# Loading the first head's K in pairs, and a running elementwise maximum, in a decode step with a gated MLP

## The chip, the cores and the metric

The kernel runs on one core of a Trainium2 chip. The metric is device time in microseconds for one execution. The span in the profile is the part from the first to the last recorded instruction of the kernel; a little time lies around it.

## The reference

One token of width 1024 goes through two branches that are mixed by a scalar gate. Branch A is attention against a long cache: 32 query heads share 4 K/V heads, 65536 cached positions, head width 128. Branch B is a small gated MLP.

```python
g = sigmoid((x * gate_w).sum(-1, keepdims=True))
# branch A
q = (x @ wq).reshape(B, Sq, 32, 128).transpose(0, 2, 1, 3)
k = repeat(k_cache, 8, axis=1)            # k_cache: (1, 4, 65536, 128), bf16
v = repeat(v_cache, 8, axis=1)
p = softmax(einsum('bhqd,bhkd->bhqk', q, k) * 128 ** -0.5)
a = einsum('bhqk,bhkd->bhqd', p, v).reshape(B, Sq, 4096) @ wo
# branch B
z = gelu(einsum('bsd,df->bsf', B_x, w_in))
z2 = layernorm(z[..., Fh:])
b = einsum('bsf,fd->bsd', z[..., :Fh] * (einsum('ts,bsf->btf', w_sp, z2) + b_sp), w_out)
out = g * a + (1 - g) * b                 # (1, 1, 1024) bf16
```

K and V are 67 MB each, so the kernel reads 162 MB from HBM in all and writes 2 KB.

## The kernel before

All large inputs pass through one SBUF tensor, `kv`, with five slots of 32 KB per partition (4 MB in all for a slot). `load` (its `dma_start` is L184) issues every one of these transfers from SP, in program order, and `load_kv(src, g, j, at, n)` loads n neighbouring tiles of K or V of head g into the slots from `at` on. A transfer waits on SP until the slots it overwrites have been read; the transfers behind it wait too. One head of K is four tiles of 4 MB, one of V is four as well. The last loop over instructions in the kernel adds an order dependence between neighbours on each engine, so that each engine runs its instructions in the order in which the program writes them.

In this text K00 to K03 are the four K tiles of head 0; K(g) h=0 and K(g) h=1 are the transfers of two K tiles of head g, and V(g) h=0 and V(g) h=1 those of V.

`k_tile(g, j, kn)` makes the scores of one K tile. In four parts, VectorE (DVE) transposes a part in place (L403, 128x2048 of int32) and TensorE (PE) multiplies it with the spread-out query `wt` (L410, 8 matmuls a part) into `s_ps`. ScalarE (ACT) copies the 128x1024 scores to a bf16 tile `sc` (L421). The tile's row maximum is taken on DVE, 128x1024 to one column of a 128x4 tile `mx` (L405); it is put into the list `late` and issued behind the first transpose of the next K tile. There are five `sc` buffers.

`stats(g)` ends the maximum of a head: the last tile's reduce (L425), the reduce over the 4 columns to `m1` (L427), a PE transpose to `mt_ps`, two small DVE steps, a PE broadcast to `nb_ps`, and `nb` (L439), minus the scaled maximum. Then ACT takes Exp of the four `sc` tiles with their sums (L443), and DVE transposes each into `pt` (L446). `v_tile(g, j, vt)` multiplies a tile of V with `pt` (L456, 32 matmuls a tile) into `o_ps`, and `head_out(g)` reduces `o_ps` to the head's part of the output vector. `build_w(g)` writes the query of head g into one of two `wt` tiles (L388, 4 DVE instructions).

The order at the start: `w_in` is loaded to slots 3 and 4, `wq` to slots 0 and 1; the MLP's first product (`z_ps`) reads the one, the query's (`q_ps`) the other. Then:

```python
    build_w(0)
    for j, n, at in ((0, 1, 2), (1, 1, 3), (2, 1, 0), (3, 1, 1)):
        for i, kn in enumerate(load_kv(A_k_cache, 0, j, at, n)):
            k_tile(0, j + i, kn)
        if j == 1:
            build_w(1)
    project(load(B_w_out.rearrange("(p c) n -> p c n", c=FC), (FC, D), 4), FC, uT, 0, first=True)
    stats(0)
```

So K00 is in slot 2, K01 in slot 3, K02 in slot 0, K03 in slot 1, the MLP's output weights in slot 4. For each head g from 1 on, the loop over h then loads a pair of K tiles of head g (slots 2 and 3 for h=0, slots 3 and 4 for h=1), makes their scores (for h=0 the second tile first, so that slot 3 comes free early), loads a pair of V tiles of head g-1 into slots 0 and 1 and multiplies them, with `stats(g)` between them for h=1. After the last head come the V tiles of head 3 and the output projection with `wo`.

Of the kernel before, what the change touches and what calls it, by code (L numbers as in the profile page):

```python
# [8 lines left out]
FP32 = mybir.dt.float32  # L9
BF16 = mybir.dt.bfloat16  # L10
I32 = mybir.dt.int32
ACT = mybir.ActivationFunctionType
ALU = mybir.AluOpType
AX = mybir.AxisListType

P = 128
CT = 128
NKV = 5
B = 32
NB = P // B  # L20
VC = 4
CC = CT // VC
# [7 lines left out]
def kernel(  # L30
# [15 lines left out]
    nc = tc.nc  # L46

    _, _, D = A_x.shape
    _, G, S, DH = A_k_cache.shape
# [9 lines left out]
    NT = S // (P * CT)  # L59
# [9 lines left out]
    wk = ctx.enter_context(tc.tile_pool(name="wk", bufs=2))  # L69
    big = ctx.enter_context(tc.tile_pool(name="big", bufs=1))  # L70
# [118 lines left out]
    def load_kv(src, g, j, at, n=1):  # L189
        h, i = divmod(j, 2)  # L190
        rows = src[0, g, 2 * h * CT * P:2 * (h + 1) * CT * P, :].rearrange(
            "(p c) d -> p (c d)", c=2 * CT)
        v = load(rows[:, i * CT * DH:(i + n) * CT * DH], (n * CT * DH,), at)
        return [v[:, i * CT * DH:(i + 1) * CT * DH] for i in range(n)]
# [115 lines left out]
    for hf in range(2):  # L310
# [30 lines left out]
                            op=ALU.subtract)  # L341
# [44 lines left out]
    def build_w(g):  # L386
        for v in range(VC):
            nc.vector.tensor_tensor(  # L388
                out=wt[g % 2][:, v, :, :, v, :],
                in0=qs[:, g].unsqueeze(2).to_broadcast([P, BP, NB, REP]),  # L390
                in1=own_n[:].unsqueeze(1).unsqueeze(3).to_broadcast([P, BP, NB, REP]),
                op=ALU.mult)
# [2 lines left out]
    late = []  # L395
    sct, ptt, mxs, lss, o_ps = {}, {}, {}, {}, {}

    def k_tile(g, j, kn):
        kb = kn.bitcast(I32)
        n = CC * DH // 2  # L400
        s_ps = pss.tile([P, 2 * HN], FP32, name="s_ps", tag="s")
        for v in range(VC):
            nc.vector.transpose(out=kb[:, v * n:(v + 1) * n], in_=kb[:, v * n:(v + 1) * n])  # L403
            while late:
                nc.vector.reduce_max(**late.pop())  # L405
            kx = kn[:, v * CC * DH:(v + 1) * CC * DH].rearrange(
                "p (c h k e) -> p h e c k", h=2, k=B, e=2)
            for b in range(BP):
                for k in range(2):
                    ins = nc.tensor.matmul(  # L410
                        s_ps[:, k * HN:(k + 1) * HN],
                        lhsT=wt[g % 2][:, v, b].rearrange("p a v h -> p (a v h)"),
                        rhs=kx[:, b // 2, b % 2, k * CC // 2:(k + 1) * CC // 2, :],
                        start=(v == 0 and b == 0), stop=(v == VC - 1 and b == BP - 1),
                        skip_group_check=True)
                    if k > 0:
                        same_weights(ins)
        if g not in mxs:
            mxs[g] = wk.tile([P, NT], FP32, name="mx")
        sct[g, j] = scp.tile([P, CC * B], BF16, name="sc")  # L420
        nc.scalar.copy(out=sct[g, j][:], in_=s_ps[:])  # L421
        late.append(dict(out=mxs[g][:, j:j + 1], in_=sct[g, j][:], axis=AX.X))

    def stats(g):
        nc.vector.reduce_max(**late.pop())  # L425
        m1 = wk.tile([P, 1], FP32, name="m1")
        nc.vector.reduce_max(out=m1[:], in_=mxs[g][:], axis=AX.X)  # L427
        mt_ps = psm.tile([1, P], FP32, name="mt_ps", tag="m")
        nc.tensor.transpose(mt_ps[:], m1[:], ident_f[:])
        gm = wk.tile([1, REP], FP32, name="gm")  # L430
        nc.vector.tensor_reduce(out=gm[:], in_=mt_ps[:].rearrange("p (a h) -> p h a", h=REP),
                                axis=AX.X, op=ALU.max)
        gr = wk.tile([1, P // REP, REP], FP32, name="gr")
        nc.vector.tensor_copy(out=gr[:], in_=gm[:].unsqueeze(1).to_broadcast([1, P // REP, REP]))
        nb_ps = psm.tile([P, 1], FP32, name="nb_ps", tag="m")
        nc.tensor.matmul(nb_ps[:], lhsT=gr[:].rearrange("p a h -> p (a h)"),
                         rhs=ones_f[0:1, 0:1], start=True, stop=True)
        nb = wk.tile([P, 1], FP32, name="nb")
        nc.vector.tensor_scalar(out=nb[:], in0=nb_ps[:], scalar1=-SCALE, scalar2=None,  # L439
                                op0=ALU.mult)  # L440
        lss[g] = wk.tile([P, NT], FP32, name="ls")
        for j in range(NT):
            nc.scalar.activation(out=sct[g, j][:], in_=sct[g, j][:], func=ACT.Exp, scale=SCALE,  # L443
                                 bias=nb[:, 0:1], accum_out=lss[g][:, j:j + 1])
            ptt[g, j] = ptp.tile([P, CC, B], BF16, name="pt")
            nc.vector.transpose(out=ptt[g, j][:].rearrange("p c x -> p (c x)"),  # L446
                                in_=sct[g, j][:])

    def v_tile(g, j, vt):
        if j == 0:  # L450
            o_ps[g] = pso.tile([P, 2, VC * DH], FP32, name="o_ps")
        vx = vt.rearrange("p (v c d) -> p c v d", v=VC, d=DH)
        for u in range(CC // 2):
            hs = slice(u % 2 * P // 2, (u % 2 + 1) * P // 2)
            for e in range(2):
                ins = nc.tensor.matmul(  # L456
                    o_ps[g][hs, e, :],
                    lhsT=ptt[g, j][:, 2 * u:2 * u + 2, :].rearrange("p c x -> p (c x)"),
                    rhs=vx[:, 2 * u + e], start=(j == 0 and u < 2),
                    stop=(j == NT - 1 and u >= CC // 2 - 2), skip_group_check=True)  # L460
                if e > 0:
                    same_weights(ins)

    def head_out(g):
        gs = slice(g * B, (g + 1) * B)
        nc.vector.tensor_tensor(  # L466
            out=om8, in0=o_ps[g][:].rearrange("p e (v d) -> p (e v) d", d=DH),
            in1=own_8[:].unsqueeze(2).to_broadcast([P, 2 * VC, DH]), op=ALU.mult)
        o_sb = wk.tile([P, DH], FP32, name="o_sb")
        nc.vector.tensor_reduce(out=o_sb[:], in_=om8.rearrange("p x d -> p d x"), axis=AX.X,  # L470
                                op=ALU.add)
        om_ps = psm.tile([P, DH + NT], FP32, name="om_ps", tag="m")
        hs = hsel[:].rearrange("p h q -> p (h q)")
        nc.tensor.matmul(om_ps[gs, DH:], lhsT=hs, rhs=lss[g][:], start=True, stop=True,
                         skip_group_check=True)
        nc.tensor.matmul(om_ps[gs, :DH], lhsT=hs, rhs=o_sb[:], start=True, stop=True,  # L476
                         skip_group_check=True)
        rl = wk.tile([P, 2], FP32, name="rl")
        nc.vector.reduce_sum(out=rl[gs, 0:1], in_=om_ps[gs, DH:], axis=AX.X)
        nc.vector.reciprocal(out=rl[gs, 1:2], in_=rl[gs, 0:1])  # L480
        om = wk.tile([P, QD, OC], FP32, name="om")
        nc.vector.tensor_tensor(
            out=om[gs], in0=om_ps[gs, :DH].rearrange("p (q c) -> p q c", c=OC),
            in1=own_q[gs, :].unsqueeze(2).to_broadcast([B, QD, OC]), op=ALU.mult)
        osum = wk.tile([P, OC], FP32, name="osum")
        nc.vector.tensor_reduce(out=osum[gs, :], in_=om[gs].rearrange("p q c -> p c q"),  # L486
                                axis=AX.X, op=ALU.add)
        nc.vector.tensor_scalar(out=oa[gs, :], in0=osum[gs, :], scalar1=rl[gs, 1:2],
                                scalar2=gate[gs, :], op0=ALU.mult, op1=ALU.mult)
# [22 lines left out]


    build_w(0)
    for j, n, at in ((0, 1, 2), (1, 1, 3), (2, 1, 0), (3, 1, 1)):
        for i, kn in enumerate(load_kv(A_k_cache, 0, j, at, n)):
            k_tile(0, j + i, kn)
        if j == 1:
            build_w(1)
    project(load(B_w_out.rearrange("(p c) n -> p c n", c=FC), (FC, D), 4), FC, uT, 0, first=True)  # L520
    stats(0)
    for g in range(1, G):
        for h in range(2):
            kn = load_kv(A_k_cache, g, 2 * h, 2 + h, 2)
            for i in ((1, 0), (0, 1))[h]:
                k_tile(g, 2 * h + i, kn[i])
            if h == 0 and g + 1 < G:
                build_w(g + 1)
            vn = load_kv(A_v_cache, g - 1, 2 * h, 0, 2)
            v_tile(g - 1, 2 * h, vn[0])  # L530
            if h == 1:
                stats(g)
            v_tile(g - 1, 2 * h + 1, vn[1])
        head_out(g - 1)
    for j, n, at in ((0, 2, 2), (2, 1, 1), (3, 1, 0)):
        for i, vt in enumerate(load_kv(A_v_cache, G - 1, j, at, n)):
# [59 lines left out]
```

## Time and profile before

| what | value |
|---|---|
| median of 4 runs | 382.32 us (382.15 to 382.48) |
| the profiled execution | 382.48 us, of which its span is 381.0 us |
| PE busy | 233.2 us (61% of the span) |
| DVE busy | 218.5 us (57%) |
| ACT busy | 39.6 us (10%) |
| DMA | 162.17 MB, 426 GB/s in the mean |

The times on each line of the profile come from one execution. Busy time is summed over an engine's instructions, and the engines work beside each other. In the slices each digit is the busy share of a fortieth of the span, in tenths. A group's row gives line, engine, operation, tile and shape, the count, then busy time and mean ns of one, then the engine's idle time ahead of it and what ended it. A timeline row gives start, duration, engine, line, operation, tile and count. Times are counted from the span's start.

### The profile page before, as it was taken

Reading aid. Unit: us, or ns where it says so; the run is one execution under the profiler, and the core shown is the slowest. Engines: PE = TensorE matmul, PEld = TensorE weight load, DVE = VectorE, ACT = ScalarE, POOL = GpSimd, SP = SyncE. Lnnn points to the kernel's source line nnn. Section 1 sums busy time; section 2 is a strip of 40 time slices with the busy share of each in tenths; the row PEclk is TensorE's granted clock in tenths of the full one; section 3 lists DMA queues with packets and bytes.
Section 4 is the critical chain, followed back from the end, with each engine's and each line's share of the span. In section 5 each row is a group of like instructions: output and inputs, shape, how many; then the busy total and the mean of one; then the engine's idle time right before and its main releaser. Section 6 shows DMA issues by size and latency. Waiting matters only on the chain.

```text
span 381.0 us, 2607 instructions
## 1 busy us (share of the span) xinstructions
PE 233.2 (61%) x1397; PEld 55.9 (15%) x800; DVE 218.5 (57%) x211; ACT 39.6 (10%) x55; POOL 4.4 (1%) x10
## 2 busy tenths in 40 slices
PE   0060557876257933786397729771977196839386
PEld 0010111111111200111011101120211021202113
DVE  4134298997597506966977059659970398460040
ACT  1001001110601100114010101050101000400000
POOL 4000000000000000000000000000000000000000
PEclk9995769899859995989688958895889579969789
DMA  9998999999999999999999999999999999999995
GB/s 385 482 440 375 408 441 437 437 475 443 414 413 413 440 435 433 433 440 440 440 435 433 440 440 433 435 420 393 440 440 435 433 420 434 440 404 440 454 408 216
DMA packets 3943, 162.17 MB, mean 426 GB/s; under 512 B 472, under 2 KB 476, under 8 KB 860
## 3 DMA queue, kind: packets, MB, share of 16 engines
q1 hardware_dynamic: 3892, 162.01, 98.7%
q8 instruction: 8, 0.13, 0.1%
q14 instruction: 3, 0.02, 0.0%
q10 hardware_dynamic: 40, 0.01, 0.0%
HBM read 162.01 MB, written 0.00 MB: 425 GB/s over the span
## 4 chain that ended last, share of the span: by engine, by line
DMA 57%; PE 26%; DVE 13%; ACT 2%; issue 1%; SPq 1%; DVEq 0%; ACTq 0%
DMA kv<-in_A_k_cache_dram 42%; PE s_ps L410 21%; DMA kv<-in_A_wo_dram 7%; DVE kv L403 7%; DMA kv<-in_A_v_cache_dram 7%; PE o_ps L456 4%; DVE pt L446 2%; DVE o_sb L470 1%; DVE mx L405 1%; ACT sc L421 1%; ACT sc L443 1%; DVE rowt L466 1%; SPq L184 1%; PE om_ps L476 0%; DVE osum L486 0%
## 5 line engine op out<-in xcount | busy, mean ns | idle before, releaser
L410 PE MATMUL s_ps<-kv,wt 128*128 128x512 bf16 x512 | 141.2, 435 | 80.8 <-DVE kv L403 80.8
L403 DVE STREAM_TRANSPOSE kv<-kv 128x2048 int32<-128x2048 int32 x64 | 142.7, 2280 | 53.5 <-DMA kv<-in_A_k_cache_dram 53.5
L456 PE MATMUL o_ps<-kv,pt 128*64 128x512 bf16 x512 | 61.9, 400 | 7.4 <-DMA kv<-in_A_v_cache_dram 7.4
L410 PEld LDWEIGHTS <-wt 128*128 128x128 bf16 x256 | 27.5, 108 | 195.7 <-issue 138.7
L421 ACT CAST sc<-s_ps 128x1024 bf16<-128x1024 f32 x16 | 16.2, 1013 | 249.9 <-PE s_ps L410 249.9
L456 PEld LDWEIGHTS <-pt 128*64 128x64 bf16 x256 | 16.1, 115 | 50.5 <-issue 48.1
L446 DVE STREAM_TRANSPOSE pt<-sc 128x1024 bf16<-128x1024 bf16 x16 | 18.6, 1217 | 6.8 <-ACT sc L443 6.8
L405 DVE TENSOR_REDUCE mx<-sc 128x1 f32<-128x1024 bf16 x12 | 14.5, 1209 | 10.7 <-ACT sc L421 10.7
L443 ACT ACTIVATE sc<-sc,nb 128x1024 bf16<-128x1024 bf16 x16 | 18.2, 1137 | 12.2 <-DVE nb L439 12.2
L466 DVE TENSOR_TENSOR rowt<-o_ps,own 128x1024 f32<-128x1024 f32 x4 | 4.8, 1194 | 24.9 <-PE o_ps L456 24.9
L476 PE MATMUL om_ps<-o_sb,hsel 128*32 128x128 f32 x8 | 2.3, 386 | 18.3 <-DVE o_sb L470 18.3
L425 DVE TENSOR_REDUCE mx<-sc 128x1 f32<-128x1024 bf16 x4 | 4.9, 1220 | 13.6 <-ACT sc L421 13.6
L296 PE MATMUL q_ps<-kv,xT 128*32 128x512 bf16 x64 | 5.7, 532 | 7.3 <-DMA kv<-in_A_wq_dram 7.3
L252 PE MATMUL xb_ps<-xg,spread 8*128 8x256 bf16 x1 | 0.4, 367 | 13.6 <-DMA xg<-in_gate_w_dram 13.6
L470 DVE TENSOR_REDUCE o_sb<-rowt 128x128 f32<-128x1024 f32 x4 | 7.5, 1871 | 0.1
L363 DVE TENSOR_TENSOR rowt<-q_ps,own_b 128x512 f32<-128x512 f32 x2 | 1.3, 686 | 10.9 <-PE q_ps L296 10.9
L495 PE MATMUL busy_ps<-wt 128*128 128x512 bf16 x25 | 6.1, 381 | 0.0
L296 PE MATMUL z_ps<-kv,xT 128*32 128x448 bf16 x64 | 6.1, 574 | 0.0
L256 DVE TENSOR_TENSOR xm<-xb_ps,sel_i 128x128 f32<-128x128 f32 x2 | 0.5, 286 | 8.4 <-PE xb_ps L252 8.4
L506 PE MATMUL out_ps<-kv,oa 128*32 128x256 bf16 x128 | 4.2, 273 | 1.7 <-DMA kv<-in_A_wo_dram 1.7
L552 ACT CAST out_sb<-out_ps 128x256 bf16<-128x256 f32 x1 | 0.4, 373 | 45.0 <-PE out_ps L506 45.0
L296 PEld LDWEIGHTS <-xT 128*32 128x32 bf16 x64 | 2.6, 138 | 14.7 <-issue 14.7
(90 smaller groups left out, 59.3 us busy)
## 6 DMA issues: line engine op xcount, KB each, us to landing
kv<-in_A_k_cache_dram SPq DMA_DIRECT2D x4, 4096.0 KB, 35.1
kv<-in_A_v_cache_dram SPq DMA_DIRECT2D x2, 4096.0 KB, 25.9
kv<-in_B_w_in_dram SPq DMA_DIRECT2D x1, 7168.0 KB, 19.9
kv<-in_A_wo_dram SPq DMA_DIRECT2D x1, 6144.0 KB
kv<-in_B_w_out_dram SPq DMA_DIRECT2D x1, 3584.0 KB
kv<-in_A_wo_dram SPq DMA_DIRECT2D x1, 1024.0 KB
kv<-in_A_wo_dram SPq DMA_DIRECT2D x1, 512.0 KB
kv<-in_A_wo_dram SPq DMA_DIRECT2D x2, 256.0 KB, 28.1
```

Of the source, the lines that this page charges most:

```text
L296: ins = nc.tensor.matmul(ps[t * B:(t + 1) * B, k * HN:k * HN + n], lhsT=xT[:, i * KH + c:i * KH + c + 1].to_broadcast([P, B]), rhs=w[:, c, ...
L403: nc.vector.transpose(out=kb[:, v * n:(v + 1) * n], in_=kb[:, v * n:(v + 1) * n])
L405: nc.vector.reduce_max(**late.pop())
L410: ins = nc.tensor.matmul(s_ps[:, k * HN:(k + 1) * HN], lhsT=wt[g % 2][:, v, b].rearrange("p a v h -> p (a v h)"), rhs=kx[:, b // 2, b % 2, ...
L421: nc.scalar.copy(out=sct[g, j][:], in_=s_ps[:])
L425: nc.vector.reduce_max(**late.pop())
L443: nc.scalar.activation(out=sct[g, j][:], in_=sct[g, j][:], func=ACT.Exp, scale=SCALE, bias=nb[:, 0:1], accum_out=lss[g][:, j:j + 1])
L446: nc.vector.transpose(out=ptt[g, j][:].rearrange("p c x -> p (c x)"), in_=sct[g, j][:])
L456: ins = nc.tensor.matmul(o_ps[g][hs, e, :], lhsT=ptt[g, j][:, 2 * u:2 * u + 2, :].rearrange("p c x -> p (c x)"), rhs=vx[:, 2 * u + e], sta ...
L466: nc.vector.tensor_tensor(out=om8, in0=o_ps[g][:].rearrange("p e (v d) -> p (e v) d", d=DH), in1=own_8[:].unsqueeze(2).to_broadcast([P, 2 ...
L470: nc.vector.tensor_reduce(out=o_sb[:], in_=om8.rearrange("p x d -> p d x"), axis=AX.X, op=ALU.add)
L495: ins = nc.tensor.matmul(ps[:, :HN], lhsT=w[:, :P], rhs=w[:, :HN], start=True, stop=True, skip_group_check=True)
```

## The change

Three edits. The four loads of head 0's K become two of 8 MB, into the slots that the tiles had before. `stats(0)` and the two V tiles of head 0 that V(0) h=0 brings move behind the first K tile of head 1, (1, 1), and ahead of its second, (1, 0); the order of the loads on SP stays. `build_w(2)`, and with it `build_w(3)`, comes after the V tiles of its half in the program. The row maximum of each tile is replaced by an elementwise maximum over the score tiles of a head, kept in a bf16 tile `mx` of 128x1024: the first tile is taken as it is, each further one costs one `tensor_tensor` with max, and `stats` reduces the result once along the row to `m1`.

```diff
+    mx = big.tile([P, CC * B], BF16, name="mx")
+
+    def running_max(g, sc):
+        if g in mxs:
+            nc.vector.tensor_tensor(out=mx[:], in0=mxs[g][:], in1=sc[:], op=ALU.max)
+            mxs[g] = mx
+        else:
+            mxs[g] = sc
+
     def k_tile(g, j, kn):
...
             while late:
-                nc.vector.reduce_max(**late.pop())
+                running_max(*late.pop())
...
-        if g not in mxs:
-            mxs[g] = wk.tile([P, NT], FP32, name="mx")
         sct[g, j] = scp.tile([P, CC * B], BF16, name="sc")
         nc.scalar.copy(out=sct[g, j][:], in_=s_ps[:])
-        late.append(dict(out=mxs[g][:, j:j + 1], in_=sct[g, j][:], axis=AX.X))
+        late.append((g, sct[g, j]))
 
     def stats(g):
-        nc.vector.reduce_max(**late.pop())
+        while late:
+            running_max(*late.pop())
         m1 = wk.tile([P, 1], FP32, name="m1")
         nc.vector.reduce_max(out=m1[:], in_=mxs[g][:], axis=AX.X)
...
     build_w(0)
-    for j, n, at in ((0, 1, 2), (1, 1, 3), (2, 1, 0), (3, 1, 1)):
-        for i, kn in enumerate(load_kv(A_k_cache, 0, j, at, n)):
+    for j, at in ((0, 2), (2, 0)):
+        for i, kn in enumerate(load_kv(A_k_cache, 0, j, at, 2)):
             k_tile(0, j + i, kn)
-        if j == 1:
+        if j == 0:
             build_w(1)
     project(load(B_w_out.rearrange("(p c) n -> p c n", c=FC), (FC, D), 4), FC, uT, 0, first=True)
-    stats(0)
     for g in range(1, G):
         for h in range(2):
             kn = load_kv(A_k_cache, g, 2 * h, 2 + h, 2)
-            for i in ((1, 0), (0, 1))[h]:
-                k_tile(g, 2 * h + i, kn[i])
-            if h == 0 and g + 1 < G:
-                build_w(g + 1)
+            first, then = ((1, 0), (0, 1))[h]
+            k_tile(g, 2 * h + first, kn[first])
+            early = g == 1 and h == 0
+            if early:
+                stats(0)
+            else:
+                k_tile(g, 2 * h + then, kn[then])
             vn = load_kv(A_v_cache, g - 1, 2 * h, 0, 2)
             v_tile(g - 1, 2 * h, vn[0])
             if h == 1:
                 stats(g)
             v_tile(g - 1, 2 * h + 1, vn[1])
+            if early:
+                k_tile(g, 2 * h + then, kn[then])
+            if h == 0 and g + 1 < G:
+                build_w(g + 1)
         head_out(g - 1)
```

## The prediction

> **What bounds the kernel now.** I read the slices and the DMA queue first, the chain of waits second, then the DMA share by windows.
>
> ```profile
> DMA  9998999999999999999999999999999999999995
> ...
> q1 hardware_dynamic: 3892, 162.01, 98.7%
> ...
> DMA 57%; PE 26%; DVE 13%; ACT 2%; issue 1%; SPq 1%; DVEq 0%; ACTq 0%
> ```
>
> The 16 DMA engines are busy from the first slice to the last but one. The chain gives PE 26% and DVE 13%, but it counts a transfer from its issue, also while earlier transfers are still moving, so its PE and DVE pieces lie beside a busy queue. Windows over the steady part settle it (last columns: PE clock, DMA share, GB/s):
>
> ```profile
> 110.00:180.00 70.00, 49.77 (x260) 10.87 (x131) 42.33 (x31) 8.69 (x12) 0.00 (x0) 0.87 1.00 434
> 180.00:260.00 80.00, 52.60 (x263) 11.47 (x135) 52.90 (x42) 8.69 (x12) 0.00 (x0) 0.82 1.00 432
> ```
>
> DMA share 1.00, while DVE is busy 42.3 of 70 us. The packet records agree: first large packet at 1.0 us, last end at 377.1; in between 16 packets are in flight throughout. So 376.1 of the 381.0 us are bytes over a fixed rate; start and tail are not edited. An edit moves the time only if it alters the rate or starves the queue.
>
> So the question at each load on SP is when it is issued, against when the queue runs dry:
>
> ```profile
> 45.37 0.44 SPq L184 DMA_DIRECT2D kv<-in_B_w_out_dram  x1
> 73.35 0.33 SPq L184 DMA_DIRECT2D kv<-in_A_k_cache_dram  x1
> 95.06 0.33 SPq L184 DMA_DIRECT2D kv<-in_A_v_cache_dram  x1
> 119.28 0.33 SPq L184 DMA_DIRECT2D kv<-in_A_k_cache_dram  x1
> ...
> 198.00 0.33 SPq L184 DMA_DIRECT2D kv<-in_A_k_cache_dram  x1
> ```
>
> By the packet records these five send their first packets at 76.7, 85.3, 104.6, 124.0 and 201.4: leads of 31, 11.9, 9.6, 4.7 and 3.4 us. 3.4 is the smallest in the kernel and costs nothing. The very first load goes out 1.0 us after issue, so about 1 us of lead is needed.
>
> [...] Before, single K tiles released the DVE at 49.87 and 59.66, about 1.1 us after their last packets at 48.85 and 58.53. [...] PE clock 0.50 in 108 to 112 us after 10 us idle; 32 matmuls then take 9.5 us, where warm ones take 1.9 per 8.
>
> **The change, part by part.** The rows used:
>
> ```profile
> L403 DVE STREAM_TRANSPOSE kv<-kv 128x2048 int32<-128x2048 int32 x64 | 142.7, 2280 | 53.5 <-DMA kv<-in_A_k_cache_dram 53.5
> ...
> L446 DVE STREAM_TRANSPOSE pt<-sc 128x1024 bf16<-128x1024 bf16 x16 | 18.6, 1217 | 6.8 <-ACT sc L443 6.8
> L405 DVE TENSOR_REDUCE mx<-sc 128x1 f32<-128x1024 bf16 x12 | 14.5, 1209 | 10.7 <-ACT sc L421 10.7
> ...
> L425 DVE TENSOR_REDUCE mx<-sc 128x1 f32<-128x1024 bf16 x4 | 4.9, 1220 | 13.6 <-ACT sc L421 13.6
> ```
>
> Maximum: 16 reduces of 1.21 us (19.4) and four small ones of 0.16 go; 12 elementwise maxima and 4 full reduces (4.9 us) come. [...] At the end of a head, stats is 0.5 to 1.1 us longer (maximum plus full reduce, against 1.22 + 0.16), but in heads 1 to 3 the PE transpose mt_ps queues behind 32 matmuls of v_tile (before: scores out at 171.0, m1 done at 172.4, mt_ps at 173.5), which cover it. Cost 0; if the cover went, at most 1.1 us off leads of 3.4 us or more.
>
> Pairs: four 4 MB loads become two of 8 MB; SP issues two instructions fewer (0.33 us each, beside the queue). Pair A (slots 2, 3) waits for the z matmuls, done at 26.6, where K00 waited for nothing; wq keeps the queue busy until 37.9. Pair B (slots 0, 1) waits for the q matmuls as before (44.9) and is due at 57.3. Leads of 11 and 12 us: no gap. Rate: packets of 32 KB took 38.06 ns/KB per engine, those of 64 KB 37.89. 16.8 MB are 1024 KB an engine: -0.17 us, between 0 and -0.3 (the best transfers, V pairs at 2.308 us/MB, against 2.325 for these four).
>
> Head 0, later: pair A lands as K01 did, so transposing starts at 59.7 instead of 49.9. Transposes in a row pace at 2.22 (four end in 8.9), so 8 end at 77.5. PE starts at 61.9, cold as before: 9.9 us for 32 matmuls, then 4 x 1.91, so 79.4. K(1) h=0 (slots 2, 3), issued at 73.35 before, goes at 79.4, due 85.3: lead 5.9. Pair B lands as K03 did, 78.6 + 0.5 to 1.0. One transpose (2.3) to 81.4-81.9, maximum to 82.1-83.1, four transposes (8.9) to 91.0-92.0. PE ends K02 1.9 us behind its last transpose, 90.7-91.7; the copy to sc 1.0, 91.8-92.8; maximum to 92.5-94.0; three transposes (6.7) to 99.2-100.7; PE to 101.1-102.6. So V(0) h=0 (slots 0, 1) goes at 101.1 to 102.6 instead of 95.06, due 104.6: lead 2.0 to 3.5 us instead of 9.6. This is the tight place. The 1 us needed leaves 1 to 2.5 us. Cost 0; each us past 103.6 would cost about one.
>
> Head 1, first half: K(1) h=0 lands at 106.9 as before. The PE is cold then in both kernels, so the maximum behind the first transpose hides and tile (1,1) ends at 119.3, as before; K(1) h=1 goes then, lead 4.7. Now stats(0): m1 at 118.4, mt_ps behind the PE's tile at 119.5, nb at 121; ACT, behind the sc copy of (1,1), loads its table (1.28) and does four Exp; the 4 pt transposes end 7.45 us after nb as before, 128.5. PE waits for V(0) h=0, landing at 126.3, and for pt, 124.9: two V tiles, cold, 9.0 us (as from 339.90 to 348.94), to 135.3. V(0) h=1 goes then, before at 137.2. Tile (1,0), queued behind them on PE and behind pt on DVE, is transposed by 137.4 and multiplied (32 matmuls, 7.6) by 142.9; before, by 130.1. Its scores are next wanted at 148.6, and its slot by K(2) h=0, which waits anyway for (1,2) at 158. build_w(2) moves with it (0.86 us, idle DVE). Nothing is issued on POOL. From 146.4 on the order is the old one[...]: leads grow or stay.
>
> Sum on the profiled execution: 382.48 (span 381.0 and 1.48 around it) - 0.17 = 382.3. The median of the runs is 382.32, 0.16 below that execution, so 382.15; I say 382.2.
>
> **The rivals.** *Starved queue (slower).* V(0) h=0 misses its due time. For it: its lead shrinks from 9.6 to about 2.7 us, below any lead that the trace shows without a gap. It decides once the issue is later than 103.6, say if the PE stays at half clock in K02 and K03 after its 2.5 us pause at 79.4 (+1.9 us for 8 matmuls, so two or three parts do it). Issue at 106.5: first packet 107.5 against engines free at 105.1 on average, 2.4 us lost, 384.7; the least harm is about 0.5, 382.8. Against: pauses of 2.3 to 2.8 us before (75.6, 86.4, 121.0) were followed by 8 matmuls in 1.9 us. Chance 0.15.
>
> *The queue gets faster.* The engines do not finish together: in the records the last is 0.9 to 2.1 us behind the mean in mid-kernel, 0.6 at the end. If the larger and fewer transfers removed that 0.6 and gave the full 0.3 of rate, 381.4. The profile speaks for the small part only. Chance 0.08, with a sliver for the chain being right that DVE time is on the path[...]; 434 GB/s at share 1.00 speaks against.
>
> [...]
>
> **The numbers.** Forecast, hidden everywhere: 0.77, alone 381.8 to 382.7. A measurement tells about 0.2%, 0.76 us, from no change: faster is below 381.56, slower above 383.08. The range reaches up into the starved case's mild half: 381.7 to 383.4. Faster 0.08, same 0.79, slower 0.13 (0.02 of the starved case stays under 0.76).
>
> **What would show it.** DMA digits 9 and q1's share near 98.7% after; K(1) h=0 issued near 79.4, V(0) h=0 at 101 to 102.6, K(1) h=1 near 119.3, V(0) h=1 near 135.3[...]. It is wrong if a DMA digit or GB/s slice dips around 104 to 107 us, if the V(0) issue is past 103.6, or if the end moves over 0.76 us with the queue full.

## The result, and the profile after

The changed kernel takes 381.88 us (median of 41 runs, 381.61 to 382.21), the kernel before 382.29 us in the same comparison (382.07 to 382.60): a ratio of 0.9988, 95% interval 0.9984 to 0.9993. It is 0.41 us faster, a tenth of a per cent. The profiled execution took 381.97 us, its span is 380.6.

The page of the changed kernel: the DMA slices, the row of the queue, the chain's shares by engine.

```profile
DMA  9999999999999999999999999999999999999995
...
q1 hardware_dynamic: 3604, 162.01, 98.7%
...
DMA 71%; PE 19%; DVE 8%; issue 1%; SPq 0%; ACTq 0%; ACT 0%; DVEq 0%
```

The queue is as full as before, with 288 packets fewer. The chain's shares moved from PE and DVE to DMA (57% of the span before, 71% now); since the queue was full both times, this says only that loads are released differently.

The windows of the changed kernel (last columns: PE clock, DMA share, GB/s) show the same rates as before, 434 and 432 GB/s at a DMA share of 1.00, though DVE is now busier in the first of them (50.1 us instead of 42.3), mostly because head 0's softmax falls into it (its `pt` transposes take 4.64 us from 122.96 on):

```profile
110.00:180.00 70.00, 50.82 (x263) 11.96 (x134) 50.12 (x40) 14.61 (x21) 0.00 (x0) 0.84 1.00 434
180.00:260.00 80.00, 49.27 (x265) 11.16 (x137) 50.14 (x39) 8.69 (x12) 0.00 (x0) 0.82 1.00 432
```

SP's timeline in the changed kernel:

```profile
78.98 0.33 SPq L184 DMA_DIRECT2D kv<-in_A_k_cache_dram  x1
100.57 0.33 SPq L184 DMA_DIRECT2D kv<-in_A_v_cache_dram  x1
118.98 0.33 SPq L184 DMA_DIRECT2D kv<-in_A_k_cache_dram  x1
135.90 0.33 SPq L184 DMA_DIRECT2D kv<-in_A_v_cache_dram  x1
```

These are K(1) h=0, V(0) h=0, K(1) h=1 and V(0) h=1. V(0) h=0 sends its first packet at 104.4: a lead of 3.8 us instead of 9.6, and no gap. The groups of the new maximum (L402 for the tiles, L435 for the reduce in `stats`):

```profile
L402 DVE TENSOR_TENSOR mx<-mx,sc 128x1024 bf16<-128x1024 bf16 x8 | 5.5, 688 | 13.9 <-ACT sc L428 13.9
L435 DVE TENSOR_REDUCE m<-mx 128x1 f32<-128x1024 bf16 x4 | 4.8, 1210 | 0.1
L402 DVE TENSOR_TENSOR mx<-sc 128x1024 bf16<-128x1024 bf16 x4 | 2.6, 650 | 0.0
```

An elementwise maximum takes 0.65 to 0.69 us, a little over half of the 1.21 us of a reduce over as many elements, and DVE is busy 211.2 us instead of 218.5. The time moved by 0.41 us, so hardly any of those 7.3 us can have come off the end; the experiments look for the rest.

### The profile page after: what moved, and what is told of

Same layout as the page of the kernel before. It is cut to its first block, busy times and chain, and to the rows that moved or that the text cites. A ratio compares the mean times of both kernels' runs of the same rounds, so it can differ in the third digit from the quotient of the medians.

```text
span 380.6 us, 2602 instructions
## 1 busy us (share of the span) xinstructions
PE 226.2 (59%) x1397; PEld 55.6 (15%) x800; DVE 211.2 (55%) x207; ACT 39.6 (10%) x55; POOL 4.4 (1%) x10
## 4 chain that ended last, share of the span: by engine, by line
DMA 71%; PE 19%; DVE 8%; issue 1%; SPq 0%; ACTq 0%; ACT 0%; DVEq 0%
DMA kv<-in_A_k_cache_dram 52%; PE s_ps L419 15%; DVE kv L412 8%; DMA kv<-in_A_wo_dram 7%; DMA kv<-in_A_v_cache_dram 7%; DMA wb<-in_B_b_sp_dram 5%; PE o_ps L464 2%; PE z_ps L296 1%; SPq L184 0%; ACTq L198 0%; PE small_ps L271 0%; ACT out_sb L566 0%; PE out_ps L514 0%; ACTq L199 0%; ACTq L201 0%
## 5 line engine op out<-in xcount | busy, mean ns | idle before, releaser
L419 PE MATMUL s_ps<-kv,wt 128*128 128x512 bf16 x512 | 132.4, 413 | 81.3 <-DVE kv L412 81.2
L464 PE MATMUL o_ps<-kv,pt 128*64 128x512 bf16 x512 | 64.4, 412 | 14.1 <-DMA kv<-in_A_v_cache_dram 14.1
L419 PEld LDWEIGHTS <-wt 128*128 128x128 bf16 x256 | 26.4, 103 | 188.7 <-issue 117.8
L464 PEld LDWEIGHTS <-pt 128*64 128x64 bf16 x256 | 17.0, 118 | 58.3 <-issue 49.6
L402 DVE TENSOR_TENSOR mx<-mx,sc 128x1024 bf16<-128x1024 bf16 x8 | 5.5, 688 | 13.9 <-ACT sc L428 13.9
L435 DVE TENSOR_REDUCE m<-mx 128x1 f32<-128x1024 bf16 x4 | 4.8, 1210 | 0.1
```

Source lines behind the costliest of these rows:

```text
L402: nc.vector.tensor_tensor(out=mx[:], in0=mxs[g][:], in1=sc[:], op=ALU.max)
L419: ins = nc.tensor.matmul(s_ps[:, k * HN:(k + 1) * HN], lhsT=wt[g % 2][:, v, b].rearrange("p a v h -> p (a v h)"), rhs=kx[:, b // 2, b % 2, ...
L464: ins = nc.tensor.matmul(o_ps[g][hs, e, :], lhsT=ptt[g, j][:, 2 * u:2 * u + 2, :].rearrange("p c x -> p (c x)"), rhs=vx[:, 2 * u + e], sta ...
```

## The experiments

The theory: the time is bytes at the rate of a full queue, so only the rate of the packets, or a load that misses its due time, moves it. The main rival: part of the 0.41 us came from less DVE work or from the new order. Medians of the kernel before were 382.24 to 382.29 us beside all of these runs; a ratio is always to the kernel before, with its 95% interval.

**Pairs alone.** The kernel before, with

```diff
-    for j, n, at in ((0, 1, 2), (1, 1, 3), (2, 1, 0), (3, 1, 1)):
-        for i, kn in enumerate(load_kv(A_k_cache, 0, j, at, n)):
+    for j, at in ((0, 2), (2, 0)):
+        for i, kn in enumerate(load_kv(A_k_cache, 0, j, at, 2)):
             k_tile(0, j + i, kn)
-        if j == 1:
+        if j == 0:
             build_w(1)
```

> The kernel before with only the four K loads of head 0 turned into two pairs; the maxima and the place of stats(0) stay. Queue theory (the time is bytes at a fixed rate, and an edit counts only through packets or through a load that misses its due time): stats(0) now ends with pt at about 113 us instead of 106.4, so tile (1,1) is multiplied by about 125.3 and K(1) h=1 is issued then, 1.3 us past the time at which the first engine runs dry (123.9); with 1 us to start, the engines lose 2 us on average: 384.1, less 0.2 to 0.4 for the packets, so 383.7 to 384.1, and a dip in the DMA near 124 to 126 us. Rival (the gain comes from the loads alone and there is slack elsewhere): 381.9, as after.

Measured: 387.10 us, ratio 1.0129 (1.0116 to 1.0143). The direction is that of the theory, but the loss is 4.8 us where 1.4 to 1.8 were expected. DVE's and PE's timelines in this kernel show what my sum had left out:

```profile
59.58 11.08 DVE L403 STREAM_TRANSPOSE kv<-kv 128x2048 int32<-128x2048 int32 x5 [10.07 <-DMA kv<-in_A_k_cache_dram]
72.85 1.22 DVE L405 TENSOR_REDUCE mx<-sc 128x1 f32<-128x1024 bf16 x1 [2.19 <-ACT sc L421]
...
61.95 11.56 PE L410 MATMUL s_ps<-kv,wt 128*128 128x512 bf16 x40 [13.76 <-DVE kv L403]
```

The reduce of K00 stands behind the first transpose of K01 and waits 2.19 us there for scores that PE makes late: it starts at half clock (the granted clock was 0.50 from 60 to 64 us, 0.56 from 64 to 68). In the changed kernel the first tile of a head costs no maximum, so DVE runs through eight transposes:

```profile
59.34 17.66 DVE L412 STREAM_TRANSPOSE kv<-kv 128x2048 int32<-128x2048 int32 x8 [10.22 <-DMA kv<-in_A_k_cache_dram]
```

With the pairs alone everything behind is late, and two loads miss their time where I had expected only K(1) h=1 to, as SP's timeline and a window of this kernel show:

```profile
82.65 0.33 SPq L184 DMA_DIRECT2D kv<-in_A_k_cache_dram  x1
105.12 0.33 SPq L184 DMA_DIRECT2D kv<-in_A_v_cache_dram  x1
127.52 0.33 SPq L184 DMA_DIRECT2D kv<-in_A_k_cache_dram  x1
```

```profile
124.00:128.00 4.00, 4.00 (x20) 0.86 (x9) 3.42 (x2) 0.47 (x1) 0.00 (x0) 1.00 0.16 66
```

These are K(1) h=0, V(0) h=0 and K(1) h=1. In the packet records V(0) h=0 starts at 106.08, 0.96 us after its issue, and takes 21.1 us from the end of the transfer before it instead of 19.4; K(1) h=1 starts at 128.47 and takes 22.4 instead of 19.5. That is about 4.7 us, most of the 5.35 us by which this profiled execution (387.83 us) is longer than that of the kernel before; the rest I did not trace. So the pairs need at least one of the two other edits. Which of them is needed is not shown: no run has the pairs with only the new maximum, or with only the moved softmax.

**Single tiles in the changed kernel.** The same diff, the other way round, on the changed kernel.

> The changed kernel with head 0's K loaded in four single tiles again; moved stats(0) and the elementwise maximum stay. Queue theory: all of the gain was in the packets of the pairs, so the time is that of the kernel before, 382.2 to 382.4. Rival (what went beyond the forecast 0.17 us comes from less DVE work or from the new order): about 382.05, half-way.

Measured: 382.08 us, ratio 0.9995 (0.9987 to 1.0003): half-way, as the rival had it. By the medians the pairs are worth about 0.20 us, and 0.2 us has another cause; differences this small lie within the interval of one run, so the packet records have to decide (below).

**The maximum alone** in the kernel before (`running_max` and its two callers, as in the change).

> The kernel before with only the maximum made elementwise. Queue theory: DVE busy falls by about 7 us and K(1) to K(3) loads are issued about 1 us earlier, the time stays: 382.2 to 382.4. Rival (DVE time is on the path as the chain of waits suggests, or fewer DVE reads make the packets faster): 381.9 to 382.1.

Measured: 382.06 us, ratio 0.9994 (0.9986 to 1.0002). The other half seemed to come with the maximum, then, and not with the order. But the packet records spoke against DVE work as its cause: packets of `wo`, 48 KB each, had 1826 ns as their 90th percentile before and 1824 here, and they move after 356 us, when no maximum is running.

**All pairs split.** In the changed kernel `load_kv` issues one load a tile:

```diff
-        v = load(rows[:, i * CT * DH:(i + n) * CT * DH], (n * CT * DH,), at)
-        return [v[:, i * CT * DH:(i + 1) * CT * DH] for i in range(n)]
+        return [load(rows[:, (i + t) * CT * DH:(i + t + 1) * CT * DH], (CT * DH,), at + t)
+                for t in range(n)]
```

> The changed kernel with all 15 pairs of K and V loaded as two single tiles, 32 KB packets instead of 64 KB: the dose for the packet size. By the medians of the packet records (1216 ns for 32 KB, 2421 for 64 KB) a pair costs 128 x 11 ns / 16 = 0.09 us more when split, so 15 cost 1.3 us: 383.2. If the whole 0.41 us of the change was the two pairs, 0.2 us a pair: 384.9. If the loads' form doesn't matter: 381.9. Two more things go with it, a half that is released earlier, which the full queue hides, and 15 more transfers.

Measured: 383.22 us, ratio 1.0023 (1.0013 to 1.0032), 1.34 us above the changed kernel; forecast 1.3. So 0.09 us a pair and 0.18 for the two of the change. Every transfer also ends with one 4-byte packet of 9 ns on each engine. In the packet records of the two profiled executions the data packets took 1.44 us an engine longer than in the changed kernel, and the 4-byte packets of the 15 added transfers 0.13 us (together 1.57, where the medians differ by 1.34): nearly all of the price is the size of the packets, not the number of transfers.

**The start of kv.** The edit of the maximum also removed two small tiles (`mx`, 128x4) from a pool that is allocated ahead of `kv`. In the allocation of the built programs `kv` starts at byte 28128 of a partition before and at 28064 after. Three runs put an unused tile ahead of it, 64 or 96 bytes in the changed kernel and 448 in the kernel before. That moves `kv` and, by the same bytes, every tile behind it, and nothing else:

```diff
+    pad = big.tile([P, 64 // 4], FP32, name="pad")
     kv = big.tile([P, NKV * CT * P], BF16, name="kv")
```

> The changed kernel with an unused tile of 64 bytes per partition ahead of kv. In the kernel before, kv starts at byte 28128 of a partition; the change took two small tiles away and it starts at 28064; here it is back at 28128. The maximum alone gave 382.06 against 382.29, and its packets were 2 to 3 ns shorter in every size class, those of wo included, which move long after the last maximum. Address theory (the start of kv sets some ns of every packet; 187 packets per engine x 1.5 ns is 0.28 us): 382.05 to 382.15. Work theory (fewer DVE reads, or chance): 381.85 to 381.95, as the changed kernel.

Measured: 382.13 us, ratio to the kernel before 0.9997 (0.9989 to 1.0004).

> The changed kernel with 96 bytes ahead of kv, so that kv starts at 28160, a multiple of 512. Address theory: packets shorter still by some ns, 381.3 to 381.8. Work theory: 381.85 to 381.95.

Measured: 380.97 us, ratio 0.9965 (0.9953 to 0.9977), 0.91 us faster than the changed kernel with the same instructions.

> The kernel before with 448 bytes ahead of kv, so that kv starts at 28576, which stands to every multiple of 512 as the changed kernel's 28064 does; nothing else is changed. Address theory: 382.0 to 382.1. Work theory: 382.29, no change.

Measured: 382.02 us, ratio 0.9994 (0.9986 to 1.0002). The two shifts by 64 bytes came out where the address theory put them, and the aligned start gained more than it had said (381.3 to 381.8). The 64 bytes moved the median by 0.25 us in the changed kernel and 0.26 in the kernel before; each interval of these two still touches 1 or the other kernel's, but the aligned start is clear of it.

Two more runs bound it: the changed kernel at 28224, a multiple of 64 but not of 128 (160 bytes of padding), and the kernel before at 28160 (32 bytes).

> The changed kernel with 160 bytes ahead of kv, so that it starts at 28224, a multiple of 64 and not of 128. With the start at a multiple of 512 it took 380.97, and packets of one size all took the same time. If a multiple of 64 is enough: 380.9 to 381.1, and 8 KB packets of 309 ns without scatter. If a larger multiple is needed: 381.3 to 382.

Measured: 381.82 us, ratio 0.9989 (0.9982 to 0.9996). This start, a multiple of 64, does not help.

> The kernel before with 32 bytes ahead of kv, so that it starts at 28160, a multiple of 512; nothing else is changed. If the start of kv acts alone, beside the pairs: the changed kernel's 380.97 at this start plus what the two pairs save there, 512 x 1213 ns against 256 x 2418 ns over 16 engines, 0.13 us: 381.1. If the elementwise maximum or the order had a part of their own: 381.3.

Measured: 381.19 us, ratio 0.9976 (0.9966 to 0.9986). The start acts without any part of the change. Beside it the change is worth 381.19 - 380.97 = 0.22 us, half-way between the two expectations, so the medians leave open whether 0.1 us is the maximum's or the order's.

The packet records settle more. Worked out from the traces: median and 90th percentile of one packet's time in ns, and in the last column the time of all data packets except those of `w_in`, in us per engine. (Those of `w_in` are the first of the kernel; their sum varies by 0.19 us from trace to trace.) "Before", "maximum alone" and "singles" load head 0's K in four tiles, the other rows in two pairs.

```
start of kv              8 KB       32 KB        48 KB        64 KB        sum
28128 before             313, 320   1216, 1224   1819, 1826   2421, 2428   358.309
28576 before             314, 321   1213, 1221   1820, 1824   2420, 2426   358.108
28064 maximum alone      314, 320   1213, 1221   1819, 1824   2421, 2426   358.105
28064 changed, singles   313, 320   1213, 1221   1819, 1824   2420, 2426   358.104
28160 before             309, 309   1213, 1213   1815, 1815   2418, 2418   357.545
28128 changed            313, 320   1216, 1224   1819, 1826   2421, 2428   358.103
28064 changed            312, 321   1218, 1221   1820, 1824   2420, 2426   357.916
28224 changed            312, 319   1215, 1222   1818, 1825   2420, 2427   357.937
28160 changed            309, 309   1213, 1213   1815, 1815   2418, 2420   357.416
```

The second, third and fourth row have the same loads, and starts that stand alike to a multiple of 512. One has the old maximum and order, one only the new maximum, one both new, and their sums agree to 0.004 us. So neither the maximum nor the order has a part in the packets' time. The step of 64 bytes is 0.20 us of packets without the pairs and 0.19 with them; the pairs are 0.19 us at 28064 and 0.13 at 28160. All these packets go into `kv`, so I put their time down to its start and not to the tiles behind it, which moved along and were not moved by themselves.

At 28160 nearly all of the scatter is gone: nine of ten packets stay within 5 ns of the least time of their class. The loss at the other starts is a few ns a packet whatever its size, so small packets lose most in share (by the medians 313 ns against 309 at 8 KB, 2421 against 2418 at 64 KB). But the start is not the whole cause. The packets of `wq`, the second load of every kernel, go into the same `kv`, and they had 2418 and 2422 ns in the kernel before at 28128 and in the changed kernel at 28064, 28224 and 28160 alike; the scatter sets in later. What must come to the start to make it cost is open.

The packets' sum also falls by less than the time. From 28064 to 28160 in the changed kernel it is 0.50 us, where the medians differ by 0.91. Most of the rest may be at the finish: in the last 3 us before the last packet's end an engine is without a packet for 1.2 us in the mean at 28064, and for 0.8 at 28160. Before the change it was 0.9, and the traces at 28064 and 28128 lie anywhere between 0.9 and 1.3, so for the change itself this can't be told.

**Number of transfers, or size of packets?** In the changed kernel each pair becomes two transfers of 64 partitions.

```diff
+        if shape == (2 * CT * DH,):
+            nc.sync.dma_start(out=v[:P // 2], in_=src[:P // 2])
+            nc.sync.dma_start(out=v[P // 2:], in_=src[P // 2:])
+            return v
```

> The changed kernel with each of the 15 pairs loaded as two transfers of 64 partitions: 15 more transfers as in the run that split all pairs, but packets of 64 KB as in the changed kernel. If the packet's size costs: 381.9 to 382.0 (the 15 more completion writes of 9 ns on each engine are 0.14 us at most). If the number of transfers costs: 383.2.

Measured: 698.69 us, ratio 1.8279 (1.8231 to 1.8326), which answers another question. A window of this kernel:

```profile
100.00:200.00 100.00, 29.18 (x158) 6.95 (x107) 42.13 (x27) 9.97 (x13) 0.00 (x0) 0.66 1.00 224
```

All DMA engines are busy, at half the rate (224 GB/s against 434 in the changed kernel); the median 64 KB packet takes 5128 ns. The next run takes the even and the odd partitions (`v[0:P:2]` and `v[1:P:2]`, and the same rows of the source) instead of the halves.

> The changed kernel with each of the 15 pairs loaded as two transfers again, one of the even and one of the odd partitions: packets of 64 KB, 15 more transfers, but each transfer reaches over all 128 partitions. The run with two halves of the partitions took 698.7 us, its 64 KB packets 5128 ns instead of 2420, so it told nothing on the number of transfers. If what halved the rate was that a transfer covers one half of the partitions, the rate is whole here, and then: packet size costs, 381.9 to 382.0; number of transfers costs, 383.2. If 64 partitions in a transfer are slow wherever they lie: near 698 again.

Measured: 577.87 us, ratio 1.5113 (1.5093 to 1.5134). The slices of this kernel:

```profile
DMA  9998039539093390399409960599139930899996
GB/s 398 466 437 375 0 150 432 255 147 437 0 437 146 147 437 0 132 423 409 201 0 437 437 291 1 220 437 437 73 146 437 433 150 1 350 419 409 427 467 259
```

Where the queue runs it runs whole, at 437 GB/s in its full slices and 2418 ns a 64 KB packet. But SP waits 429 us for DVE's transposes, in the changed kernel 156, loads are issued much later (the second K pair at 79.8 us instead of about 45), and the queue stands empty. So its time is no measure, and its packets are a weak one: `kv` starts at 28064 here too, yet 48 KB packets took 1815 ns at the median and at the 90th percentile, as at 28160. With pauses in the queue most of the scatter is gone, so this run can't be set against a full queue. What speaks for the packet's size is the sum of packets in the split of all pairs; a time that separates the two is missing.

**A load made late.** The changed kernel, with six needless DVE operations in K03:

```diff
+            for _ in range(6 if (g, j, v) == (0, 3, 1) else 0):
+                nc.vector.tensor_tensor(out=rowt[:], in0=rowt[:], in1=rowt[:], op=ALU.max)
```

> The changed kernel with six needless elementwise operations of about 1.17 us on DVE (128x1024, fp32) in the last K tile of head 0, so that V(0) h=0 is issued 7.0 us later, at 107.6 instead of 100.57. Queue theory: its first packet goes 0.96 us after issue (so in the run with pairs alone, 105.12 to 106.08), 108.5, while the engines were free at 104.8 on average: 3.7 us lost, 385.6, with one late load only and the rest in its old leads. If DVE or PE time were on the path: 388.9. If there is slack elsewhere: 381.9.

Measured: 388.72 us, ratio 1.0170 (1.0156 to 1.0183), near the number I had given for a path through DVE (388.9). The time alone would speak for that path; the profile decides otherwise. From SP's timeline, PE's timeline and a window:

```profile
110.34 0.33 SPq L184 DMA_DIRECT2D kv<-in_A_v_cache_dram  x1
```

```profile
104.41 5.91 PE L421 MATMUL s_ps<-kv,wt 128*128 128x512 bf16 x16 [7.73 <-DVE kv L412]
```

```profile
104.00:108.00 4.00, 3.60 (x9) 0.58 (x4) 3.41 (x3) 0.00 (x0) 0.00 (x0) 0.50 0.04 16
```

The load went out at 110.3, not 107.6: the six operations took 7.5 us in a row, PE was idle for 7.7 us behind the added operations, and its next 16 matmuls took 5.9 us, at a clock of 0.50 from 104 to 108 us, instead of 3.8. The first packet went 0.97 us after issue, and this transfer took 26.8 us from the end of the one before, 7.4 more than in the changed kernel. By the packet records the engines stood empty for 6.8 us in the mean, and their first packets then took 3.02 us in the mean instead of 2.42. The profiled execution is 389.44 us, 7.5 above that of the changed kernel. So the loss is the hole in the queue and 0.6 us for starting again, which my sum had at nothing; the larger part of my error was the issue time.

## Why the prediction was right

The forecast was 382.2 us, hidden everywhere, with the move inside 0.2%; measured were 381.88. The queue never ran dry, and the loads stood where the ledger put them: K(1) h=0 at 78.98 (forecast 79.4), V(0) h=0 at 100.57 (101.1 to 102.6), K(1) h=1 at 118.98 (119.3), V(0) h=1 at 135.90 (135.3). No trace of the kernel before has an elementwise maximum, so the time the forecast gave one, in its ranges for `stats` and for the steps of K02, was my estimate and not shown there; the changed kernel has 0.65 to 0.69 us and DVE busy for 211.2. By the groups above, `stats` ends with 0.69 + 1.21 us where it had 1.22 + 0.16, so it is 0.5 us longer.

The pairs' -0.17 us was right: 0.18 by the split of all 15, 0.20 by single tiles in the changed kernel, 0.19 by the sum of the packets.

The term that was mis-sized is the rate. The sum counted packet size alone, -0.17, and the measured move is -0.41. Of the rest, 0.20 us is packet time that goes with the start of `kv`, 64 bytes lower because the edit of the maximum gave up two small tiles. The ledger had no line for where a destination lies, and that the start moved to the better side was luck. The packets left nothing for DVE time or the order, so the sliver of a chance that the chain was right about DVE fell. The rival of an evener finish is not refuted: at 28160 the engines wait about 0.4 us less at the end, though that came with the start and not with larger transfers, and a small part of it in the change's own 0.41 is not excluded.

The starved queue did not occur, but its place and its mechanism were shown by runs. V(0) h=0 is the tight load. It had its first packet 0.96 to 0.97 us after its issue in the two runs where it was late, and the engines come free from 104.4 on, at 104.8 in the mean: by these numbers I estimate that an issue past 103.4 begins to lose, past 103.8 by the mean (I had said 103.6). In the run with the late load, 6.5 us past 103.8 left the engines empty for 6.8 us, about one for one, and starting again cost 0.6 more (first packets of 3.02 us instead of 2.42). The profile's own margin was about 3 us. What would have decided it was half clock on PE, which I had named (0.50 from 60 to 64 us with the pairs alone), and DVE waiting for the first tile's scores (2.19 us there), which I had not.

That PE kept its clock in K02 and K03 was in part luck. I had argued from three pauses of 2.3 to 2.8 us after which 8 matmuls took 1.9 us, and had left a fourth of the same length out. It stands first here, from the kernel before, and the pause in the changed kernel second:

```profile
66.28 7.04 PE L410 MATMUL s_ps<-kv,wt 128*128 128x512 bf16 x24 [2.35 <-DVE kv L403]
...
81.13 1.91 PE L419 MATMUL s_ps<-kv,wt 128*128 128x512 bf16 x8 [2.19 <-DVE kv L412]
```

The first 24 matmuls took 7.0 us where three groups of 8 with pauses of 0.3 between them take 6.3, and the clock was 0.66 from 68 to 72 us. With the pairs alone the same happened at 98.05, 7.04 us for 24 matmuls, again after 2.37 us. In the kernel before, a pause of 2.36 us ahead of 88.75 was followed by 8 matmuls in 1.89 us. So the pause's length does not tell the two cases apart in these traces, and how long a pause PE bears at full clock was not shown. Another reading was off without harm: single K tiles released DVE about 0.5 us after the last packet of their transfer (the 4-byte one, at 49.41 and 59.13), not 1.1. That pair A lands only as a whole held: in the changed kernel DVE begins on the first pair at 59.34, after its last data packet at 58.85.

The rate stayed where it had been, 434 and 432 GB/s in the windows before and after; that it is fixed, with no room above it, was my estimate, and no run shows a ceiling. Nor does any run show why the start of `kv` costs, or which boundary counts: none tried a start that is a multiple of 128 or 256 and not of 512.

## What to carry to other kernels

Where the DMA queue is full all the way, make a ledger of load issues against the times at which the queue would run dry, with the notice a load needs, and price every edit by it. Busy time on other engines was worth nothing here while the leads held: DVE was busy 7.3 us less, and the packets' sum with the new maximum and with the old one, at starts alike to a multiple of 512, was 358.105 and 358.108 us. Then look at the packets: large ones (0.09 us a pair here), and where the destination starts. The one start at a multiple of 512 bytes that was tried, 28160, gave 0.91 us here for 96 bytes of padding, twice what the whole change gave, and the fastest kernel of this study, 380.97 us. And when an edit changes what is allocated, look up whether the large buffers moved before explaining a small difference by the work.

## What the runs showed of the hardware that I had not expected

- Where the destination started in SBUF went with some ns of each packet while the queue stayed full: nine of ten 8 KB packets took 309 ns at 28160, and up to 320 at 28128. It did not change the second load of the kernel (2418 and 2422 ns at every start), nor the 48 KB packets of a kernel whose queue had pauses (1815 ns at 28064).
- Loads of 64 neighbouring partitions, from 64 neighbouring rows, ran at about half the rate: 224 GB/s and 5128 ns a 64 KB packet, while loads of every second partition and row had 2418 ns. Whether the source or the destination is the slow side was not separated.
- A load of all partitions into an empty queue sent its first packet 0.95 to 0.97 us after its issue on SP, in three cases (1.26 with every second partition), and the first packet of each engine took about 3.0 us instead of 2.42.
